# Loads of the first queries and key differences moved among the projections, hi and lo in one store, keys of two heads from ScalarE's queue

## The chip, the cores and the metric

The kernel runs on one core of a Trainium2 chip. The metric is the device time of one execution in microseconds. Three timed runs of the kernel before gave 1366.81, 1367.34 and 1368.3 us, a median of 1367.34.

## What is computed

The reference joins two results for a sequence of 2048 rows of 448 numbers, side by side. The first half is a state-space convolution: a kernel K is summed from complex exponentials and applied to `u` by FFT. The second half is attention with 16 heads of 28:

```python
K = 2.0 * jnp.einsum("dn,dnl->dl", C, P).real
y = jnp.fft.irfft(Uf * Kf[None, :, :], L2)[:, :, :L]        # then + u * D_skip
...
qkv = (x @ wqkv).reshape(B, S, 3, H, Dh).transpose(2, 0, 3, 1, 4)
scores = jnp.einsum("bhqd,bhkd->bhqk", q, k) * scale
o = jnp.einsum("bhqk,bhkd->bhqd", softmax(scores), v)
b = o.transpose(0, 2, 1, 3).reshape(B, S, D) @ wo
```

## The kernel before

The work has two parts. In the first (`for t in range(n_stage)`, line 515, 41 steps) the projections of `x` are computed beside the seeds of the exponentials. In the second (`for s in range(NS)`, line 980) attention, the powers of the exponentials and the FFT of the convolution run interleaved in an order written out by hand (`ORDER`, line 33).

**Projections.** `x` comes in four chunks of 512 rows (`load_x`, `transposes`). `qk_proj(c, s, g)` (line 440) multiplies chunk c by the weights of group g (four heads) for the keys (s = 1) or the queries (s = 0), in three products of split numbers each, 12 matmuls in all. Its result stands in one of three PSUM tiles (`w_tile`). The function `evac` that it returns splits the result: ScalarE writes the rounded part `th` (hi), VectorE the rest `tl` (lo), and SP stores both in DRAM, `k_d` or `q_d`. For the keys of the first two chunks it also makes the differences of two halves, `dh` and `dl`, and stores them in `kd_d`. There are 32 such jobs and 16 of `v_proj` (line 474). `project` (line 507) starts a job and then evacuates the one before it; PW = 37 spreads the 48 jobs over the first 37 steps. For the last chunk the v jobs come first, and then keys and queries of groups 0 to 3 by turns.

**Seeds.** `seeds(o)` (line 308), eight of them, four steps apart (SP = 4), each go through GpSimd, VectorE and ScalarE: `phases`, `reduce`, `sines`, `sizes`, `g_base`, `g_first` and so on. Their products `sg` and `se` are stored in `sd_d` (`put_g`, `put_e`). `se` is a buffer of the ring `qhat` with three buffers, which the queries use too (`places`, line 354).

**Loads for attention.** After the last projection (t + 1 == PW) the pool of the weights is closed (`wst.close()`, line 522) and the key pools are opened where it was. Then SP issues, in this order: `load_q(0)`, and for each of four heads `load_kd(0, j)` and `load_k(0, j)`; then `load_q(1)` and four `load_v`. Each of `load_k` (line 140), `load_kd` (line 154) and `load_q` (line 159) consists of four DMAs, one for each 32 partitions.

**First maxima.** Then the row maxima of the first 512 queries are computed (`max_mm`, line 166): 16 blocks, each with four matmuls. The first uses the key differences; ScalarE takes its positive part into `rl` (a tile of the pool `kd_p`), and VectorE joins it with the second and reduces the other two. `max_join`, `max_end` and `max_put` write the maximum into the queries, and the second part begins.

**Order.** In the first part the program's order on each engine is set by a scheduler at build time, which moves instructions; in the second, everything stays in the order written. SP issues DMAs in its order. Each DMA signals one of eight completion counters, taken in turn, and waits for the DMA that had this counter before.

Of the kernel before, what the change touches and what calls it, by code (L numbers as in the profile page):

```python
# [1 line left out]

# [5 lines left out]
F32 = mybir.dt.float32  # L8
F32R = mybir.dt.float32r
# [13 lines left out]
HG = H // G  # L23
CQ = 512
# [15 lines left out]
PS = 1  # L40
SGB, XB, XL = 2, 5, 4
K0, KP, KD, UP = 0, 3.5, 5, 3

N1 = 32
N2 = 64
# [43 lines left out]
def body(ctx, tc, a, out):  # L89
    nc = Engines(tc)  # L90
# [29 lines left out]
    att, k0_st = ExitStack(), ExitStack()  # L120
    ps_w, n_ring = [None, 3], [0]

    def w_tile():

        n_ring[0] += 1
        return ps_w[0].tile([128, CQ], F32, name=f"pm{n_ring[0] % ps_w[1]}")

    q_p = pool(att, "q_p", side="right")
    v_p = pool(att, "v_p", side="right")

    def mm32(o, w, x_, start, stop, at=0):

        for i in range(w.shape[-1] // 32):
            c = slice(32 * i, 32 * i + 32)
            nc.tensor.matmul(o[c], w[:, c], x_, start=start, stop=stop, tile_position=(0, at + 32 * i))


    kt_g, kd_g, q_u, m_u, mh_u, o_u, rl_u = {}, {}, {}, {}, {}, {}, {}

    def load_k(g, j, p):  # L140
        t = p.tile([128, L], F32R, name="khat", bufs=HG)
        for r in range(4):
            nc.sync.dma_start(t[32 * r:32 * r + 32, :].bitcast(F32), k_d[g][r % 2, 32 * j:32 * j + 32, :])
        kt_g.setdefault(g, []).append(t)

    v_g = {}
# [1 line left out]
    def load_v(g, c):  # L148
        v_g[g, c] = t = v_p.tile([128, NK // NQ, HG, 32], F32, name="v", bufs=5)
        nc.sync.dma_start(t.rearrange("p t h e -> p t (h e)"), v_d[c][:, g])  # L150

    kd_p = [None]

    def load_kd(g, j):
        kd_g[g, j] = t = kd_p[0].tile([128, CQ], F32R, name=f"kdif{j}")
        for r in range(4):
            nc.sync.dma_start(t[32 * r:32 * r + 32].bitcast(F32), kd_d[g][r % 2, 32 * j:32 * j + 32, :])

    def load_q(u):
        g, c = divmod(u, NQ)  # L160
        t = q_p.tile([128, HG, CQ], F32R, name="qhat", bufs=3)
        for r in range(4):
            nc.sync.dma_start(t[32 * r:32 * r + 32].bitcast(F32), q_d[g][c][r // 2].rearrange("(j p) q -> p j q", j=HG))
        q_u[u] = t

    def max_mm(u, i, kc, ps=w_tile):

        if i == 0 and kc == 0:
            m_u[u] = q_p.tile([128, HG, 4, 3], F32, name="mx", bufs=2)
        j, t = divmod(i, 4)  # L170
        pm = ps()
        q, kt = q_u[u][:, j, t * 128:(t + 1) * 128], kt_g[u // NQ][j]
        mx = m_u[u][:, j, t, max(kc - 1, 0):max(kc - 1, 0) + 1]
        if kc == 0:
            nc.tensor.matmul(pm, q, kd_g[u // NQ, j], start=True, stop=True)
            rl_u[u, i] = kd_p[0].tile([128, CQ], F32, name="rl", bufs=2)
            nc.scalar.activation(rl_u[u, i], pm, AF.Relu)
        elif kc == 1:
            kb = kt.rearrange("p (c s n) -> p c s n", c=NQ, s=2)[:, :2, 1, :]
            nc.tensor.matmul(pm.rearrange("p (c n) -> p c n", c=2), q, kb, start=True, stop=True)  # L180
            rl = rl_u.pop((u, i))
            nc.vector.tensor_tensor_reduce(rl, pm, rl, 1.0, -3.0e38, ALU.add, ALU.max, mx)
        else:
            nc.tensor.matmul(pm, q, kt[:, kc * CQ:(kc + 1) * CQ], start=True, stop=True)
            nc.vector.tensor_reduce(mx, pm, axis=AX.X, op=ALU.max)
# [19 lines left out]
    with ExitStack() as st:  # L205
# [3 lines left out]
        x_p = pool(xst, "x_p")  # L209
        y_p = pool(wst, "y_p", side="right")  # L210
# [45 lines left out]
        t = a["A_log_dt"]  # L256
# [183 lines left out]
        def qk_proj(c, s, g):  # L440
            pp = w_tile()
            hs = slice(HG * g, HG * g + HG)
            n = 0
            for k in range(NCK):
                for w_, x_ in ((wh, xh), (wl, xh), (wh, xl)):
                    nc.tensor.matmul(pp, w_[:, s, k, hs, :].rearrange("p h e -> p (h e)"), x_[k],
                                     start=n == 0, stop=n == 3 * NCK - 1)
                    n += 1

            def evac():  # L450
                th = x_p.tile([128, CQ], F32R, name="th", bufs=2)
                tl = x_p.tile([128, CQ], F32R, name="tl", bufs=2)
                if s == 1:
                    nc.scalar.activation(th, pp, AF.Identity, bias=kones)
                    nc.vector.scalar_tensor_tensor(tl, pp, kones, th.bitcast(F32), op0=ALU.add, op1=ALU.subtract)
                else:
                    nc.scalar.activation(th, pp, AF.Copy)
                    nc.vector.tensor_tensor(tl, pp, th.bitcast(F32), ALU.subtract)
                if s == 1 and c < 2:
                    HC = CQ // 2  # L460
                    kb = y_p.tile([128, HC], F32, name="kb")
                    dh = y_p.tile([128, HC], F32R, name="dh")
                    dl = y_p.tile([128, HC], F32R, name="dl")
                    nc.scalar.activation(kb, pp[:, HC:], AF.Copy)
                    nc.vector.tensor_tensor(kb, pp[:, :HC], kb, ALU.subtract)
                    nc.scalar.activation(dh, kb, AF.Copy)
                    nc.gpsimd.tensor_tensor(dl, kb, dh.bitcast(F32), ALU.subtract)
                    for i, t in enumerate((dh, dl)):
                        nc.sync.dma_start(kd_d[g][i, :, c * HC:(c + 1) * HC], t.bitcast(F32))
                for i, t in enumerate((th, tl)):  # L470
                    nc.sync.dma_start(k_d[g][i, :, c * CQ:(c + 1) * CQ] if s == 1 else q_d[g][c][i], t.bitcast(F32))
            return evac

        def v_proj(c, t):
# [25 lines left out]
        slots = [[] for _ in range(n_stage)]  # L500
# [3 lines left out]
        slots[1].insert(0, turn_dt)  # L504
        pend, n_work = [], len(work)

        def project():

            e = work.pop(0)() if work else None
            while pend:  # L510
                pend.pop(0)()
            if e:
                pend.append(e)

        for t in range(n_stage):
            while work and n_work - len(work) < n_work * (t + 1) / PW:
                project()
            for f in slots[t]:
                f()
            if t + 1 == PW:  # L520
                project()
                wst.close()
                kd_p[0] = pool(att, "kd_p", side="right")
                k0_p = pool(k0_st, "k0_p", side="right")
                load_q(0)
                for j in range(HG):
                    load_kd(0, j)
                    load_k(0, j, k0_p)
                load_q(1)
                for c in range(NQ):  # L530
                    load_v(0, c)
# [188 lines left out]
    def fin(u, s_):  # L720
# [15 lines left out]
        def scale():  # L736
            pw = w_tile()
            for t in range(4):
                mm32(pw[:, t * 128:(t + 1) * 128], rb[:, t].rearrange("p h e -> p (h e)"), ident, True, True)
            nc.vector.tensor_tensor(on, o, pw, ALU.mult)  # L740
            if g < G - 1:
                nc.sync.dma_start(on_d[c][g], on)
            else:
                p_due.extend((s_ + PD + PS * t, lambda t=t: project(t)) for t in range(4))
# [107 lines left out]
        for kc in range(4):  # L852
            max_mm(1, i, kc)

    import collections
    urgent, back = collections.deque(), collections.deque()
    powers = {"g": collections.deque(), "e": collections.deque()}
    done = {"mm": -1}
# [121 lines left out]
    for s in range(NS):  # L980
        u, kt = divmod(s, NK)
# [57 lines left out]
    s = NS  # L1039
# [63 lines left out]
```

## Time and profile before

| what | value |
|---|---|
| median of three timed runs | 1367.34 us |
| the profiled execution | 1366.65 us |
| its span, first to last instruction | 1364.9 us |
| busy: PE, DVE, ACT, POOL | 1243.5, 980.3, 968.6, 831.0 us |
| mean granted clock of TensorE | 0.975 |
| DMA moved | 205.37 MB, mean 150 GB/s |

The page gives busy time by engine, the same in 40 slices of the span with the granted clock, the chain of work that ended last, and the costliest groups of instructions. All of the program's operations are recorded by one helper, so that they all have line 73; they are told apart by the names of their tiles: `th` and `tl` for the evacuations, `qhat`, `kdif` and `khat` for the loaded queries, key differences and keys, `mx` for the maxima, `tri`, `sg` and `px` for the seeds. SPq is the queue SP, with the DMAs that it issues.

### The profile page before, as it was taken

What the parts mean: (1) busy time and instruction counts of PE and PEld (TensorE: products, weight loads), DVE (VectorE), ACT (ScalarE), POOL (GpSimd) and SP (SyncE); (2) the same over time, 40 slices, a digit from 0 to 9 for tenths busy, and PEclk for the clock granted to TensorE, in tenths of its full rate; (3) what the DMA queues carried; (4) which work ended last, traced back from release to release, by engine and by line L of the source; (5) the groups of instructions that cost most, each with busy time, mean ns of one, the idle gap of its engine ahead of it and who ended that gap; (6) DMA issues with size and microseconds to landing.
All of it is one profiled execution on the core that took longest, in us unless ns stands there. A gap on an engine that the chain in (4) does not pass through costs nothing.

```text
span 1364.9 us, 33230 instructions
## 1 busy us (share of the span) xinstructions
PE 1243.5 (91%) x12625; PEld 707.2 (52%) x12625; DVE 980.3 (72%) x2138; ACT 968.6 (71%) x2069; POOL 831.0 (61%) x705
## 2 busy tenths in 40 slices
PE   6978784799999999999999999999998999998997
PEld 4866662355555555555555555555555545544433
DVE  5778765877777777777788888887887766857311
ACT  4867662488888888888888888878786665655553
POOL 3576661187877877878878988888896111202221
PEclk9988896999999999999999999999999999999999
DMA  6775679726675546378533233632324544636476
GB/s 194 241 243 193 219 263 246 208 62 140 160 168 119 131 125 155 109 205 209 161 96 88 64 72 78 148 86 66 77 66 139 181 123 154 208 109 205 138 192 178
DMA packets 200729, 205.37 MB, mean 150 GB/s; under 512 B 96632, under 2 KB 159160, under 8 KB 198520
## 3 DMA queue, kind: packets, MB, share of 16 engines
q1 hardware_dynamic: 200568, 203.23, 53.5%
q8 instruction: 100, 1.64, 0.5%
q14 instruction: 61, 0.50, 0.1%
HBM read 120.73 MB, written 82.18 MB: 149 GB/s over the span
## 4 chain that ended last, share of the span: by engine, by line
PE 58%; DVE 16%; ACT 11%; POOL 5%; DMA 5%; issue 3%; SPq 0%; ACTq 0%; DVEq 0%; POOLq 0%
PE pm L73 34%; PE po L73 13%; PE pss L73 12%; ACT p L73 6%; DVE mx L73 3%; POOL qhat L73 3%; DVE g L73 2%; ACT rl L73 2%; DVE p L73 2%; DMA khat<-k 2%; DVE tri L73 1%; DVE pr L73 1%; DVE px L73 1%; POOL x_e L73 1%; DVE sg L73 1%
## 5 line engine op out<-in xcount | busy, mean ns | idle before, releaser
L73 ACT ACTIVATE p<-pss 128x512 f32<-128x512 f32 x1024 | 565.3, 608 | 137.0 <-PE pss L73 128.4
L73 PE MATMUL pss<-qhat,khat 128*128 128x512 f32 x1024 | 402.2, 399 | 3.5 <-ACT p L73 3.4
L73 DVE TENSOR_REDUCE mx<-pm 128x1 f32<-128x512 f32 x500 | 321.4, 683 | 104.6 <-PE pm L73 103.4
L73 PE MATMUL pm<-khat,qhat 128*128 128x512 f32 x749 | 329.7, 443 | 41.5 <-DVE mx L73 36.1
L73 POOL TENSOR_TENSOR e<-e,sdb 128x256 f32<-128x256 f32 x168 | 201.9, 1202 | 166.0 <-ACT e L73 157.0
L73 PE MATMUL po<-p,v 128*32 128x512 f32 x2048 | 271.8, 598 | 0.0
L73 POOL TENSOR_TENSOR e<-e,eu 128x256 f32<-128x256 f32 x168 | 248.5, 1479 | 13.2
L73 PEld LDWEIGHTS pm<-khat,qhat 128*128 128x128 f32 x749 | 141.0, 189 | 217.7 <-DVE mx L73 83.4
L73 PEld LDWEIGHTS pss<-qhat,khat 128*128 128x128 f32 x1024 | 190.6, 188 | 45.9 <-issue 11.1
L73 DVE CUSTOM_DVE_ANT_0 rl<-pm,rl 128x512 f32<-128x512 f32 x249 | 171.5, 689 | 47.3 <-ACT rl L73 44.2
L73 POOL TENSOR_TENSOR eu<-e,sdb 128x256 f32<-128x256 f32 x168 | 201.8, 1201 | 0.0
L73 DVE TENSOR_TENSOR g<-g,zg 128x128 f32<-128x128 f32 x392 | 162.9, 416 | 46.6 <-ACT zg L73 41.5
L73 ACT ACTIVATE rl<-pm 128x512 f32<-128x512 f32 x249 | 150.8, 606 | 24.9 <-PE pm L73 24.9
L73 POOL TENSOR_TENSOR p<-pr,pr 64x448 f32<-64x448 f32 x32 | 40.9, 1277 | 191.7 <-DVE pr L73 180.6
L73 PE MATMUL pm<-kdif,qhat 128*128 128x512 f32 x249 | 100.9, 405 | 2.4 <-DMA v<-v 1.3
L73 PEld LDWEIGHTS pm<-e,g 128*32 128x32 f32 x3584 | 63.0, 110 | 52.8 <-issue 30.9
L73 DVE TENSOR_TENSOR zg<-g,zg 128x128 f32<-128x128 f32 x224 | 87.5, 391 | 1.9
L73 PEld LDWEIGHTS po<-p,v 128*32 128x32 f32 x2048 | 56.5, 110 | 42.6 <-issue 37.9
L73 PE MATMUL pm<-e,g 128*32 128x64 f32 x3584 | 72.5, 220 | 0.0
L73 ACT ACTIVATE y<-pm 128x448 f32<-128x448 f32 x48 | 26.3, 548 | 63.5 <-PE pm L73 30.9
L73 PE MATMUL pm<-xh,wh 112*128 112x512 f32 x128 | 56.2, 443 | 11.2 <-DVE tl L73 5.1
L73 DVE TENSOR_TENSOR pr<-pm,ub 128x448 f32<-128x448 f32 x64 | 37.0, 619 | 32.7 <-PE pm L73 32.7
(137 smaller groups left out, 1555.4 us busy)
## 6 DMA issues: line engine op xcount, KB each, us to landing
sdb<-sd SPq DMA_DIRECT2D x56, 336.0 KB
qhat<-q SPq DMA_DIRECT2D x64, 256.0 KB
khat<-k SPq DMA_DIRECT2D x64, 256.0 KB
sd<-sg SPq DMA_DIRECT2D x8, 1456.0 KB
mw<-in_mw SPq DMA_DIRECT2D x16, 512.0 KB
sd<-qhat SPq DMA_DIRECT2D x8, 896.0 KB
yk<-yk SPq DMA_DIRECT2D x56, 128.0 KB
yu_d<-ub SPq DMA_DIRECT2D x64, 112.0 KB
```

The costliest lines, as they stand in the source:

```text
L73: i = f(*args, **kw)
```

## The change

Four edits. The pool `kd_p` is opened at the start, with room of its own, so that `load_kd` can be called before the weights' pool is closed. The 16 DMAs of the first group's key differences are issued two at a time in steps 26 to 33, and the four of the first queries in steps 34 and 35. Hi and lo share one tile, `hl` (differences: `dhl`), and go out in one DMA of twice the size. The keys of heads 0 and 1 of the first group are issued by ScalarE, those of heads 2 and 3 by SP as before.

```diff
+A0, A1 = 26, 34
...
+    kd_p = pool(att, "kd_p", side="right")
...
-    def load_k(g, j, p):
+    def load_k(g, j, p, queue=nc.sync):
         t = p.tile([128, L], F32R, name="khat", bufs=HG)
         for r in range(4):
-            nc.sync.dma_start(t[32 * r:32 * r + 32, :].bitcast(F32), k_d[g][r % 2, 32 * j:32 * j + 32, :])
+            queue.dma_start(t[32 * r:32 * r + 32, :].bitcast(F32), k_d[g][r % 2, 32 * j:32 * j + 32, :])
...
-    def load_kd(g, j):
-        kd_g[g, j] = t = kd_p[0].tile([128, CQ], F32R, name=f"kdif{j}")
-        for r in range(4):
+    def load_kd(g, j, rows=range(4)):
+        if 0 in rows:
+            kd_g[g, j] = kd_p.tile([128, CQ], F32R, name=f"kdif{j}")
+        t = kd_g[g, j]
+        for r in rows:
...
-    def load_q(u):
+    def load_q(u, rows=range(4)):
...
-                th = x_p.tile([128, CQ], F32R, name="th", bufs=2)
-                tl = x_p.tile([128, CQ], F32R, name="tl", bufs=2)
+                hl = x_p.tile([128, 2, CQ], F32R, name="hl", bufs=2)
+                th, tl = hl[:, 0], hl[:, 1]
...
-                    for i, t in enumerate((dh, dl)):
-                        nc.sync.dma_start(kd_d[g][i, :, c * HC:(c + 1) * HC], t.bitcast(F32))
-                for i, t in enumerate((th, tl)):
-                    nc.sync.dma_start(k_d[g][i, :, c * CQ:(c + 1) * CQ] if s == 1 else q_d[g][c][i], t.bitcast(F32))
+                    nc.sync.dma_start(kd_d[g][:, :, c * HC:(c + 1) * HC].rearrange("i p l -> p i l"), dhl.bitcast(F32))
+                nc.sync.dma_start((k_d[g][:, :, c * CQ:(c + 1) * CQ] if s == 1 else q_d[g][c]).rearrange("i p l -> p i l"),
+                                  hl.bitcast(F32))
...
+        ahead = collections.defaultdict(list)
+        for i in range(2 * HG):
+            ahead[A0 + i].append(lambda i=i: load_kd(0, i // 2, range(2 * (i % 2), 2 * (i % 2) + 2)))
+        for i in range(2):
+            ahead[A1 + i].append(lambda i=i: load_q(0, range(2 * i, 2 * i + 2)))
...
-            for f in slots[t]:
+            for f in slots[t] + ahead.get(t, []):
                 f()
             if t + 1 == PW:
                 project()
                 wst.close()
-                kd_p[0] = pool(att, "kd_p", side="right")
                 k0_p = pool(k0_st, "k0_p", side="right")
-                load_q(0)
                 for j in range(HG):
-                    load_kd(0, j)
-                    load_k(0, j, k0_p)
+                    load_k(0, j, k0_p, nc.scalar if j < 2 else nc.sync)
                 load_q(1)
```

More of the change, by code (lines that the diff above doesn't have):

```diff
@@ L1 @@
+import collections
 from contextlib import ExitStack
@@ L150, in load_v @@
         nc.sync.dma_start(t.rearrange("p t h e -> p t (h e)"), v_d[c][:, g])
-    kd_p = [None]
-    def load_kd(g, j):
-        kd_g[g, j] = t = kd_p[0].tile([128, CQ], F32R, name=f"kdif{j}")
-        for r in range(4):
+    def load_kd(g, j, rows=range(4)):
[3 more added lines that the diff above has]
+        for r in rows:
             nc.sync.dma_start(t[32 * r:32 * r + 32].bitcast(F32), kd_d[g][r % 2, 32 * j:32 * j + 32, :])
-    def load_q(u):
+    def load_q(u, rows=range(4)):
         g, c = divmod(u, NQ)
-        t = q_p.tile([128, HG, CQ], F32R, name="qhat", bufs=3)
-        for r in range(4):
+        if 0 in rows:
+            q_u[u] = q_p.tile([128, HG, CQ], F32R, name="qhat", bufs=3)
+        t = q_u[u]
+        for r in rows:
             nc.sync.dma_start(t[32 * r:32 * r + 32].bitcast(F32), q_d[g][c][r // 2].rearrange("(j p) q -> p j q", j=HG))
-        q_u[u] = t
     def max_mm(u, i, kc, ps=w_tile):
@@ L175, in max_mm @@
             nc.tensor.matmul(pm, q, kd_g[u // NQ, j], start=True, stop=True)
-            rl_u[u, i] = kd_p[0].tile([128, CQ], F32, name="rl", bufs=2)
+            rl_u[u, i] = kd_p.tile([128, CQ], F32, name="rl", bufs=2)
             nc.scalar.activation(rl_u[u, i], pm, AF.Relu)
@@ L461, in evac @@
                     kb = y_p.tile([128, HC], F32, name="kb")
-                    dh = y_p.tile([128, HC], F32R, name="dh")
-                    dl = y_p.tile([128, HC], F32R, name="dl")
+                    dhl = y_p.tile([128, 2, HC], F32R, name="dhl")
+                    dh, dl = dhl[:, 0], dhl[:, 1]
                     nc.scalar.activation(kb, pp[:, HC:], AF.Copy)
@@ L853, in body @@
             max_mm(1, i, kc)
-    import collections
     urgent, back = collections.deque(), collections.deque()
```

## The prediction

> **What bounds the kernel now.** I read the page first (span and slices), then the busy time by stretch, and then the timeline of the stretch where the slices show a hole.
>
> ```profile
> span 1364.9 us, 33230 instructions
> PE   6978784799999999999999999999998999998997
> PEclk9988896999999999999999999999999999999999
> ```
>
> From the ninth slice on TensorE is at 9 tenths in almost every slice, with an order written out by hand that the change doesn't touch. I take that part, from about 255 us to the end, as a block that starts earlier or later and keeps its length. The first eight slices (34 us each) are not full, and the hole is in the seventh (4 tenths, the clock at 6). Busy time by stretch (columns: stretch and its length, PE, PEld, DVE, ACT, POOL busy with counts, granted clock, DMA share, GB/s):
>
> ```profile
> 180.00:200.00 20.00, 18.64 (x71) 14.31 (x71) 15.35 (x29) 14.09 (x30) 12.20 (x17) 0.91 0.93 322
> 200.00:212.00 12.00, 0.00 (x0) 0.00 (x0) 7.73 (x19) 2.24 (x7) 5.42 (x9) 0.69 0.53 182
> 212.00:224.00 12.00, 1.62 (x3) 0.93 (x4) 0.00 (x0) 1.08 (x2) 4.18 (x5) 0.50 1.05 250
> 224.00:238.00 14.00, 12.52 (x31) 6.24 (x31) 13.18 (x29) 3.58 (x6) 0.00 (x0) 0.84 1.04 237
> ```
>
> TensorE does nothing from 200 to 212 us and almost nothing to 224, while the DMA engines are full from 212 on. The timeline says who waits (start, duration, engine, operation; in brackets the idle time before and what ended it):
>
> ```profile
> 199.23 0.40 PE L73 MATMUL pm<-xl,wh 112*128 112x512 f32 x1
> 201.65 0.66 POOL L73 TENSOR_TENSOR tri<-tri 128x224 f32<-128x224 f32 x1
> 202.34 0.56 DVE L73 TENSOR_TENSOR sg<-pn,tri 128x224 f32<-128x224 f32 x1 [5.25 <-POOL tri L73]
> 206.95 0.55 DVE L73 TENSOR_TENSOR sg<-sg,px 128x224 f32<-128x224 f32 x1
> 207.69 0.68 ACT L73 ACTIVATE th<-pm,kones 128x512 fp32r<-128x512 f32 x1
> 210.84 0.32 SPq L73 DMA_DIRECT2D q<-tl  x1
> 211.22 1.87 SPq L73 DMA_DIRECT2D qhat<-q  x4
> 213.18 1.76 SPq L73 DMA_DIRECT2D kdif<-kd  x4
> 215.04 3.23 SPq L73 DMA_DIRECT2D khat<-k  x4
> 219.17 0.79 PE L73 MATMUL pt<-kdif,qhat 128*128 128x512 f32 x1 [19.54 <-DMA kdif<-kd]
> 223.60 0.76 PE L73 MATMUL pt<-khat,qhat 128*128 128x512 f32 x1 [3.20 <-DMA khat<-k]
> 224.52 0.69 DVE L73 CUSTOM_DVE_ANT_0 rl<-pt,rl 128x512 f32<-128x512 f32 x1 [13.44 <-PE pt L73]
> 246.74 0.50 PE L73 MATMUL pm<-kdif,qhat 128*128 128x512 f32 x1 [1.30 <-DMA v<-v]
> 254.97 0.20 DVE L73 TENSOR_REDUCE m<-mx 128x16 f32<-128x48 f32 x1
> ```
>
> The last projection is multiplied by 199.6, but ScalarE copies it out only at 207.7: it stands behind the copies of the last seed (`sg`), these behind VectorE's chain (202.34 to 207.50), and that behind GpSimd's `tri`. The last stores are issued until 210.84, and only then the queue SP reaches the loads. The maxima start on VectorE at 224.52 and end at 254.97; they are VectorE's pace, 48 passes in 30.45 us, with one stall of 1.3 us for a load. So the stretch that the change works on is 199 to 224.5, and what counts is the time of that first maximum.
>
> **The change part by part.** It was made against the built order of both programs (which instruction stands behind which on each engine, and which completion it waits for), with durations of this profile. The profiled execution took 1366.65 us, 1.75 over its span; the median of the three timed runs is 1367.34. My sum is made against 1366.65.
>
> *First queries and key differences earlier.*
>
> ```profile
> qhat<-q SPq DMA_DIRECT2D x64, 256.0 KB
> kdif<-kd SPq DMA_DIRECT2D x16, 64.0 KB
> sd<-sg SPq DMA_DIRECT2D x8, 1456.0 KB
> sd<-qhat SPq DMA_DIRECT2D x8, 896.0 KB
> 193.07 0.37 SPq L73 DMA_DIRECT2D sd<-sg  x1
> 203.86 0.39 SPq L73 DMA_DIRECT2D sd<-qhat  x1
> ```
>
> 4 issues (1.87 us) and 16 issues (1.76 each four) leave the hole for earlier places on SP. Of what stood ahead of the first head's keys, the issues from 211.22 to 215.04, 3.8 us, go. Their 2.1 MB (4 x 256 and 16 x 64 KB) move earlier: at the 250 GB/s of the row from 212 on that is 8.4 us of transfer, in a stretch that ends with a DMA share of 0.93 (180 to 200). The cover is the DMA engines' idle share; where it is gone, stores land later, and that is the last item of this part. Two things spoil the gain. The last two quarters of the queries don't get away: the DMAs take eight completion counters in turn, and the third quarter has the counter of the first key piece, so it is issued only when that has landed. And the stores of the last seed but one, 2.4 MB that are issued at 193.07 and 203.86 now, stand in the new order of SP behind the stores of the last projections but two, so they fall into the hole. At the 322 GB/s of 180 to 200 they take 7.5 us there.
>
> *Keys by ScalarE.* In the built order the first two pieces of head 0 stand before ScalarE's last two evacuations, the third between them, the fourth and head 1 after. The first waits for the last-but-one multiplication of the last projection, whose weights lie where the keys go. Behind it on ScalarE are two evacuations and the `rl` copies; the first maxima wait for those, and for the keys anyway.
>
> *What moves with it.* In the new order the evacuations of the last four projections are behind the last seed's copies too, so TensorE can't finish at 199.6: the last projection needs the PSUM tile that is freed by the third evacuation from the end. Clock and pitch for that:
>
> ```profile
> 202.00:204.00 2.00, 0.00 (x0) 1.00 0.00 0
> 226.00:228.00 2.00, 2.00 (x6) 0.50 0.98 206
> 228.00:230.00 2.00, 1.89 (x6) 0.91 1.11 286
> 196.90 0.40 PE L73 MATMUL pm<-xh,wl 112*128 112x512 f32 x1
> ```
>
> Eleven matmuls from 196.90 to 199.23 are 0.233 us apart; the granted clock is still 1.00 at 202 to 204, 0.50 from 212 on (row above), and back only at 228, four us after the steady work began. Now step by step. GpSimd's `tri` comes before the seed's other products in the new order (two of 0.40 and one of 0.42 stood ahead of it), so 201.65 becomes about 200.4 and it ends at 201.1. VectorE's chain of 5.2 us (202.34 to 207.50) then ends at 206.3, with the evacuation that frees the last-but-one projection inside it, at about 205.5. That projection runs cold, 12 x 0.46 = 5.5 us, to 211.0; the last, whose tile is free by 208.5, runs 12 x 0.233 = 2.8 us warm, to 213.8. Both pitches are the 0.233, at half clock doubled. First key piece at 213.9 and second, 0.32 each as a lone issue; evacuation 0.68; third piece; evacuation; fourth piece issued by 216.5. It lands 3.2 us later if it goes as a lone store does (136.42 to 139.66 in the rows below), or 5.3 later as the fourth piece does now (issued by 218.27, used at 223.60). VectorE follows 0.9 after that (223.60 to 224.52). That gives a first maximum at 220.6 or 222.7, against 224.52. Now 2.3 MB are issued in the 7 us up to that piece; in the new order it is some 3 MB in 8 us (two merged stores, the seed's 1.5 MB, half of the queries, the keys). So I take a value nearer to the late end, 222.0: 2.5 us earlier. The stall of 1.3 us goes as well: the fourth head's keys have 2.1 MB of loads fewer ahead of them, and each head feeds VectorE for 7 us. **Gain in the hole: 3.8 us**; ends 5.2 (early landing, stall gone) and 1.8 (late landing, stall stays).
>
> *One store for hi and lo.* 64 stores of keys and queries and 16 of differences become 40: 40 x 0.32 = 12.8 us less of SP, which is not on the chain. What it costs is a wait. The two halves share one tile of two buffers, so ScalarE's hi of the next but one projection waits for a store that waits for VectorE's lo. Now hi waits for hi alone:
>
> ```profile
> 70.54 0.60 ACT L73 ACTIVATE th<-pm 128x512 fp32r<-128x512 f32 x1
> 72.16 0.38 SPq L73 DMA_DIRECT2D q<-tl  x1
> 134.25 0.32 SPq L73 DMA_DIRECT2D q<-tl  x1
> 135.40 0.58 ACT L73 ACTIVATE th<-pm 128x512 fp32r<-128x512 f32 x1
> 136.42 0.94 SPq L73 DMA_DIRECT2D k<-th  x1
> 138.35 0.47 SPq L73 DMA_DIRECT2D k<-tl  x1
> 138.71 0.69 DVE L73 TENSOR_TENSOR tl<-pm,th 128x512 fp32r<-128x512 f32 x1 [0.85 <-DMA q<-tl]
> 139.66 0.69 ACT L73 ACTIVATE th<-pm,kones 128x512 fp32r<-128x512 f32 x1 [0.43 <-DMA k<-th]
> ```
>
> Two landing times stand here: 3.2 us (136.42 to 139.66) and 4.4 (134.25 to 138.7). The hi at 70.54 would have to wait for the lo stored at 72.16, that is to 76.6 at most, 6.0 us; that at 135.40 to 138.7, 3.3; that at 139.66 to 141.6, 1.9. Bounds: about 11 us of held ScalarE if all lands on the chain, nothing if its idle time takes it (it is busy 14.09 of 20 us in the row above). Behind a held hi stand the sines and copies of the seeds, on which GpSimd and VectorE wait. The nearest row is that of the table of waits from 18 to 215 us:
>
> ```profile
> ACT th L73 <- DMA k<-th: 1.4, 2, 0.9
> ```
>
> This is what ScalarE loses by stores of hi today (total, times, longest). **I take 1.4 us more**, this loss once again: the pairs at 70 and 135 us are the worst that I found, and ScalarE has idle time behind them.
>
> **Sum:** 1366.65 - 3.8 + 1.4 = 1364.25, so 1364.2 us, 3.1 under the median shown.
>
> The Trainium skill has a rule against one edit (DMA: Bandwidth & Descriptors, "Issuing engines are not separate DMA queues"): transfers from ScalarE and SP run on the same 16 DMA engines and interleave, so a second issuer saves issue time alone. The DMA share of 1.05 and 1.04 in the rows from 212 to 238 agrees; by that rule the keys of heads 2 and 3 could slow head 0. In the built order they stand behind the last store and behind pieces of heads 0 and 1, so my sum has no term for it; its result is the first rival.
>
> **Rivals.**
>
> 1. *The hole only changes its owner.* Keys still can't leave before the last projection is done, which is then 14 us later than 199.6; the last query quarters wait behind the first key piece, the seed's stores fill the DMA engines, and the stall in the loop stays. First maximum at 222.7: 1366.65 - 1.8 + 1.4 = 1366.2, no difference. For it speaks that the DMA engines are full from 212 on already; against it, that 2.1 MB of what fills them are moved away. That the first queries aren't loaded ahead as the change says is a part of this case.
>
> 2. *The merged store holds ScalarE (slower).* Place: the bursts of projections about 70 and 135 us; price up to 11.2 us, against a gain of 3.8. It decides from 7.3 us on: 1366.65 - 3.8 + 7.3 = 1370.1; at the full price 1374.0. For it: GpSimd's, VectorE's and ScalarE's parts of a seed form one chain with no slack at 202 (5.25 us of VectorE waiting for GpSimd), and ScalarE runs in order. Against it: ScalarE has 6 of 20 us idle (14.09 busy), and the like waits cost 1.4 us now.
>
> **How the numbers follow.** A measurement of this kernel can tell about 0.2% (2.7 us) from no change: faster is below 1364.6, slower above 1370.1. My forecast has 0.52, with its own range of 1360.5 (the early end of the gain, and a microsecond from the shorter SP queue) to 1366.2; 0.43 of it lies below 1364.6, since the late landing is in its value already, and 0.09 above. Rival 1 has 0.14, all of it within 0.2%. Rival 2 has 0.34, all of it above 1370.1. That makes 0.43, 0.23 and 0.34. The range goes from 1359.5, for a phase that also gets shorter by the 40 issues saved, to 1372.5, which takes in the nearer two thirds of rival 2.
>
> **What would show it.** Right: the first maximum on VectorE at 222 plus the 1.4 us of held ScalarE, no stall near the fourth head, `m<-mx` at about 252.6. TensorE's last projections cold and about ten us later than now, with `khat` issued by ScalarE between the last evacuations. Wrong: GpSimd's last `tri` later than 201.65 (then the projections, not the hole, took the time; look at ScalarE's waits for stores), or a first maximum that is earlier but a loop that stalls (rival 1). If the stretch from 255 us on changes its length, my block assumption fails.

## The result: 5.4 us slower, and the profile after

The changed kernel takes 1372.21 us, the median of ten runs (1368.84 to 1375.94), beside 1366.79 for ten runs of the kernel before. The ratio is 1.0036, with a 95% interval of 1.0025 to 1.0047. The profiled execution took 1372.32 us. The ratio is the one on record; it isn't the plain quotient of the two medians.

The page of the changed kernel: the span, TensorE's busy tenths and its granted clock.

```profile
span 1370.5 us, 33146 instructions
PE   7877775799999999999999999999998999998997
PEclk9988986899999999999999999999999999999999
```

The hole in the seventh slice is still there, a little less deep (5 tenths for 4). Busy time of the four stretches that the prediction showed (columns as there):

```profile
180.00:200.00 20.00, 16.22 (x67) 12.62 (x65) 13.90 (x28) 13.91 (x24) 12.47 (x16) 0.91 0.52 178
200.00:212.00 12.00, 6.25 (x21) 4.98 (x22) 8.82 (x21) 4.05 (x14) 5.55 (x11) 0.72 0.76 247
212.00:224.00 12.00, 1.07 (x5) 0.54 (x3) 1.44 (x2) 1.28 (x2) 5.24 (x6) 0.66 1.03 309
224.00:238.00 14.00, 10.20 (x21) 5.68 (x21) 7.98 (x17) 3.19 (x6) 0.00 (x0) 0.56 1.06 296
```

TensorE now works from 200 to 212 us (the last projections), as foreseen. But the DMA engines are full until 238 as before, now at 309 and 296 GB/s where it was 250 and 237: bytes were to leave the hole, and more are in it. VectorE has 7.98 us of work from 224 to 238, where it had 13.18. The timeline of the changed kernel (ACTq is the queue ScalarE):

```profile
200.75 0.65 POOL L75 TENSOR_TENSOR tri<-tri 128x224 f32<-128x224 f32 x1
205.75 0.79 PE L75 MATMUL pm<-xh,wh 112*128 112x512 f32 x1 [5.97 <-DVE hl L75]
210.47 0.50 SPq L75 DMA_DIRECT2D sd<-sg  x1
212.67 0.40 PE L75 MATMUL pm<-xl,wh 112*128 112x512 f32 x1
212.87 1.56 ACTq L75 DMA_DIRECT2D khat<-k  x2
214.56 1.10 ACTq L75 DMA_DIRECT2D khat<-k  x1
215.81 10.24 ACTq L75 DMA_DIRECT2D khat<-k  x5
219.83 1.02 SPq L75 DMA_DIRECT2D qhat<-q  x2
227.25 0.77 PE L75 MATMUL pt<-kdif,qhat 128*128 128x512 f32 x1 [14.18 <-DMA khat<-k]
228.91 1.29 DVE L75 TENSOR_REDUCE mx<-pm 128x1 f32<-128x512 f32 x2 [11.81 <-PE pm L75]
252.05 0.50 PE L75 MATMUL pm<-kdif,qhat 128*128 128x512 f32 x1 [1.31 <-DMA v<-v]
260.28 0.20 DVE L75 TENSOR_REDUCE m<-mx 128x16 f32<-128x48 f32 x1
```

Up to 213 us this is the prediction within about a microsecond. Then the 1456-KB store of the last seed but one (`sd<-sg`) goes out 2.4 us ahead of the first key piece. That piece, issued at 212.87, has landed by 219.83, since the third query quarter, which waits for its counter, is issued then: 7.0 us. The last two quarters are needed at 227.25, some 7 us after their issue. (The row names `khat` as what ended the wait, but this matmul reads `kdif` and `qhat`. The trace also holds the time of every counter's increments: by them the first key piece was complete at 219.81, the fourth at 223.28, and the last query quarter, issued at 220.52, at 227.01. So the queries end the wait, whatever the row names.) The first maximum is at 228.91 in place of 224.52, 4.4 us later; the stall of 1.3 us for a load (252.05) is still there; the loop ends 5.3 us later (260.28 for 254.97); the span is 5.6 us longer.

Behind the loop both kernels do the same work. Busy time by stretch there, first of the kernel before, then of the changed one (the third figure from the right is the granted clock):

```profile
254.00:260.00 6.00, 4.41 (x10) 2.20 (x10) 4.41 (x12) 1.20 (x2) 0.00 (x0) 0.72 0.26 76
260.00:266.00 6.00, 4.79 (x14) 2.18 (x14) 3.79 (x9) 4.08 (x8) 0.00 (x0) 1.00 0.84 215
266.00:272.00 6.00, 4.54 (x27) 2.03 (x26) 5.90 (x14) 4.82 (x11) 5.41 (x7) 1.00 0.67 140
1234.00:1240.00 6.00, 5.85 (x46) 2.89 (x47) 2.35 (x6) 1.85 (x4) 0.00 (x0) 0.72 0.26 66
```

```profile
260.00:266.00 6.00, 5.46 (x11) 2.79 (x11) 4.42 (x12) 1.19 (x2) 0.00 (x0) 0.51 0.37 112
266.00:272.00 6.00, 5.73 (x14) 3.33 (x13) 3.21 (x8) 4.20 (x9) 0.00 (x0) 0.63 0.83 195
272.00:278.00 6.00, 4.63 (x16) 2.15 (x17) 4.67 (x12) 3.34 (x8) 5.53 (x7) 0.72 0.60 123
1234.00:1240.00 6.00, 4.02 (x40) 1.99 (x38) 5.06 (x8) 3.53 (x7) 3.83 (x3) 1.00 1.04 374
```

The changed kernel runs cold for longer after the loop (0.51, 0.63, 0.72), and the same ScalarE instructions, matched one by one, are then 7.4 us behind instead of 5.3; near 1235 us the kernel before falls to half clock once (0.72) and the changed one doesn't, and 1.7 us come back. What I took for a block has joints.

### The profile page after: what moved, and what is told of

Same layout as the page of the kernel before. It is cut to its first block, busy times and chain, and to the rows that moved or that the text cites. A ratio compares the mean times of both kernels' runs of the same rounds, so it can differ in the third digit from the quotient of the medians.

```text
span 1370.5 us, 33146 instructions
## 1 busy us (share of the span) xinstructions
PE 1242.8 (91%) x12625; PEld 709.0 (52%) x12625; DVE 990.5 (72%) x2138; ACT 969.2 (71%) x2069; POOL 824.7 (60%) x705
## 4 chain that ended last, share of the span: by engine, by line
PE 61%; DVE 16%; ACT 11%; DMA 4%; issue 3%; POOL 3%; SPq 0%; ACTq 0%; DVEq 0%; POOLq 0%
PE pm L75 36%; PE po L75 13%; PE pss L75 12%; ACT p L75 6%; DVE mx L75 3%; DVE tri L75 2%; DVE g L75 2%; ACT rl L75 2%; DVE p L75 2%; POOL qhat L75 2%; DVE pr L75 1%; DMA khat<-k 1%; DVE sg L75 1%; DVE px L75 1%; DVE zg L75 1%
## 5 line engine op out<-in xcount | busy, mean ns | idle before, releaser
L75 ACT ACTIVATE y<-pm 128x448 f32<-128x448 f32 x48 | 26.3, 547 | 62.0 <-issue 30.3
```

The lines of the kernel that those rows point to most:

```text
L75: i = f(*args, **kw)
```

## The experiments

Three theories stood at the start. **Store:** the 1456-KB store ahead of the keys fills the DMA engines, so that everything behind it lands late. **Counter:** the last two query quarters wait for a key piece's counter. **Merged store** (second rival of the prediction): the shared tile holds ScalarE. A fourth came with the first traces: **held VectorE**, below. All results (times in us; *tri* is the start of GpSimd's last triangle product, *first* that of VectorE's first maximum, *end* that of `m<-mx`, all in the profiled execution; *rest* is span minus *end*; *cold* the time at half clock in the rest, in the trace's clock record, where each stretch that lies wholly in it is a multiple of 3.4 us). The medians of e1 to e14 come from three chips, on which the kernel before made 1366.97 to 1367.63; the ratio compares runs of one chip and is the better guide:

| kernel | median | ratio to before, 95% | tri | first | end | rest | cold |
|---|---|---|---|---|---|---|---|
| before | 1366.79 | | 201.65 | 224.52 | 254.97 | 1109.9 | 10.2 |
| changed | 1372.21 | 1.0025 to 1.0047 | 200.75 | 228.91 | 260.28 | 1110.2 | 18.0 |
| e1 queries earlier | 1375.88 | 1.0050 to 1.0092 | 197.11 | 225.79 | 258.58 | 1111.8 | 19.8 |
| e2 stores deferred | 1366.50 | 0.9984 to 1.0009 | 198.61 | 222.65 | 252.99 | 1110.1 | 10.3 |
| e3 keys by SP | 1373.42 | 1.0035 to 1.0059 | 197.94 | 229.18 | 259.63 | 1112.8 | 20.5 |
| e4 before + merged store | 1373.85 | 1.0030 to 1.0056 | 205.00 | 231.53 | 261.99 | 1112.1 | 19.8 |
| e5 clamp from PSUM | 1372.55 | 1.0023 to 1.0052 | 196.44 | 224.86 | 256.71 | 1114.0 | 20.5 |
| e6 e2 + e5 | 1362.45 | 0.9956 to 0.9979 | 195.56 | 218.72 | 249.07 | 1111.6 | 16.0 |
| e7 two stores again | 1374.66 | 1.0044 to 1.0070 | 200.84 | 230.37 | 261.94 | 1112.8 | 20.5 |
| e8 changed, again | 1371.64 (one) | | 198.33 | 227.16 | 258.66 | 1111.1 | 18.8 |
| e9 short seed store | 1365.24 | 0.9989 to 1.0009 | 201.56 | 225.57 | 255.91 | 1110.2 | 16.5 |
| e10 before + early loads | 1375.98 | 1.0052 to 1.0079 | 199.89 | 232.09 | 262.55 | 1112.1 | 20.0 |
| e11 before + ScalarE's keys | 1368.15 | 1.0000 to 1.0017 | 200.12 | 221.89 | 254.17 | 1109.9 | 14.0 |
| e12 before + clamp from PSUM | 1368.13 | 0.9995 to 1.0015 | 200.22 | 224.87 | 255.72 | 1110.6 | 16.5 |
| e13 e4 + clamp from PSUM | 1363.78 | 0.9956 to 0.9980 | 199.52 | 221.62 | 252.08 | 1110.0 | 10.2 |
| e14 e9 + clamp from PSUM | 1366.20 | 0.9974 to 1.0000 | 198.40 | 222.49 | 252.83 | 1113.5 | 20.5 |

Every edit lets the build-time scheduler order the first part anew, so a variant is never the edit alone; where the order matters, the text says so.

### e1: the counter alone

```diff
-A0, A1 = 26, 34
+A0, A1 = 26, 30
```

> The changed kernel with the four pieces of the first queries issued in steps 30 and 31 in place of 34 and 35. In the built order all four are then ahead of the first key piece, and none has its completion counter. Main theory (the last two query quarters are issued only when the first key piece has landed, 219.8 us, and the first maximum waits for them): the first maximum then waits for head 0's keys alone, which were complete at about 223.3, so it comes at about 224.3 in place of 228.9, and the time is 1372.2 - 4.6 = 1367.6 us. Second theory (the 1456-KB store ahead of the keys decides, through bytes alone): the first key piece still takes about 7 us to land, 219 to 220, and the first maximum is between 224 and 227. Rival (the merged store of hi and lo takes the time before 213): nothing moves, first maximum at 229, 1372.

The queries were there in time, and the median is 3.7 us above that of the changed kernel, where 4.6 less was expected. The six executions go from 1372.19 to 1382.79, and the profiled one is the fastest of them. The timeline of e1:

```profile
207.65 0.44 SPq L75 DMA_DIRECT2D sd<-sg  x1
213.12 1.66 ACTq L75 DMA_DIRECT2D khat<-k  x2
215.39 0.69 ACT L75 ACTIVATE hl<-pm,kones 128x512 fp32r<-128x512 f32 x1 [5.93 <-DMA k<-hl]
216.70 11.33 ACTq L75 DMA_DIRECT2D khat<-k  x6
224.99 0.77 PE L75 MATMUL pt<-khat,qhat 128*128 128x512 f32 x1 [6.14 <-DMA khat<-k]
```

The first maximum now waits for the keys. Their second half is issued only at 216.70, since ScalarE's evacuation ahead of it waits until 215.39 for a merged store that was issued at 209.18 behind the seed's store, and it lands 8 us later. From *tri* to *first* it is 28.7 us, in the changed kernel 28.2. But *tri* is a poor start for the hole: the first key piece is issued 16.0 us after it in e1 (213.12) and 12.1 in the changed kernel (212.87). From that issue to *first* it is 12.7 us in e1 and 16.0 in the changed kernel. So the counter is worth some 3 us of the hole itself, although both stores of the seed stand ahead of the keys in e1; this order lost them again ahead of the hole and in the loop (*first* to *end* 32.8 for 31.4).

### e2 and e9: the store

e2 issues both stores of that seed behind the keys of all heads:

```diff
+        held = slots[SP * 6 + 11][:1] + slots[SP * 6 + 12][:1]
+        del slots[SP * 6 + 11][:1], slots[SP * 6 + 12][:1]
...
                     load_k(0, j, k0_p, nc.scalar if j < 2 else nc.sync)
+                for f in held:
+                    f()
                 load_q(1)
```

> The changed kernel with the two stores of the last seed but one (1456 and 896 KB) issued after the loads of all four heads' keys. The queries' third and fourth quarter get other counters by it; the fourth key piece gets that of the first. Store theory (the 1456-KB store that is issued 2.4 us ahead of the first key piece holds the DMA engines): the first key piece lands 3 to 4 us after its issue in place of 6.9, at about 216.5; the fourth is issued at about that time and lands by 220; first maximum at 221, time 1364.5. If only the shared counter matters and the landing stays at 7 us: the fourth key piece is issued at 219.8 and lands at 224 to 226, first maximum at 225 to 227, time 1368 to 1370. Rival (merged store): 1372.

e9 leaves the store in its place and makes it a third (the rest of that seed's `sg` is left out, and the second part reads the seed before it in its place):

```diff
-            put_g = lambda: nc.sync.dma_start(sd_d[o][:, :, F_G:].rearrange("b p f -> p b f"), q["sg"])
+            put_g = lambda w=128 if o == 6 else None: nc.sync.dma_start((sd_d[o][:, :, F_G:F_G + w] if w else sd_d[o][:, :, F_G:]).rearrange("b p f -> p b f"),
+                                              q["sg"][:, :, :w] if w else q["sg"])
...
-        nc.sync.dma_start(sds[b], sd_d[b // BO][b % BO])
+        nc.sync.dma_start(sds[b], sd_d[5 if b // BO == 6 else b // BO][b % BO])
```

> The changed kernel, but of the last seed but one only 128 of 364 columns of sg are stored (512 KB in place of 1456), and the second part reads the seed before it in its place; work is left out by that, and the result is another one. The store stays where it is, ahead of the keys; the last two query quarters get counters of the queries' first quarter and of a store. Theory of the store's bytes: key pieces land in under 5 us as with the deferred stores (6.9 us in the changed kernel), GpSimd's last triangle product to first maximum 24 to 25 us (28.2 and 28.8 in two profiles of the changed kernel), time 1366 to 1369. If the place of the store or its counter matters and not its bytes: 28 us and 1372.

The two timelines, e2 first:

```profile
208.33 1.61 SPq L75 DMA_DIRECT2D qhat<-q  x2
211.86 0.82 ACTq L75 DMA_DIRECT2D khat<-k  x2
216.68 3.90 ACTq L75 DMA_DIRECT2D khat<-k  x5
221.42 0.77 PE L75 MATMUL pt<-khat,qhat 128*128 128x512 f32 x1 [5.40 <-DMA khat<-k]
```

```profile
211.28 0.55 SPq L75 DMA_DIRECT2D sd<-sg  x1
211.88 2.70 SPq L75 DMA_DIRECT2D qhat<-q  x2
215.13 0.83 ACTq L75 DMA_DIRECT2D khat<-k  x2
220.90 3.01 ACTq L75 DMA_DIRECT2D khat<-k  x5
224.34 0.77 PE L75 MATMUL pt<-khat,qhat 128*128 128x512 f32 x1 [3.73 <-DMA khat<-k]
```

In both the fourth key piece has the first one's counter, so its issue shows the first landing: 4.8 us after issue in e2 (211.86 to 216.68), 5.8 in e9. Then 4.7 and 3.4 us until TensorE reads them. Two landings in a row again, but shorter ones: from *tri* to *first* 24.0 us in both, 4.2 less than in the changed kernel, the stall in the loop is gone (*first* to *end* 30.3 against 31.4), and the time goes from 1372.2 to 1366.5 and 1365.2. In e2 the fourth key piece's wait for the first one's counter kept the first maximum at 222.65, not the 221 of the store theory.

**The store theory is not shown by these two alone.** In both, the last two query quarters also got other counters and went out ahead of the keys (the `qhat` rows above), so the counter's part is in their gain too. And the second profile of the changed kernel, e8, speaks against the bytes of the first landing:

```profile
208.06 0.52 SPq L75 DMA_DIRECT2D sd<-sg  x1
211.92 1.57 ACTq L75 DMA_DIRECT2D khat<-k  x2
217.73 1.02 SPq L75 DMA_DIRECT2D qhat<-q  x2
```

With the whole 1456 KB issued 3.9 us ahead, the first key piece landed in 5.8 us (counter record), and with 512 KB 3.9 us ahead, in e9, in 5.7; e6, with neither store ahead, has 6.2. The nine profiles with early queries and ScalarE's keys sort better by the counter. From the issue of the first key piece to *first* it is 15.2 to 16.9 us where the last quarters wait for it (changed kernel, e5, e7, e8), 12.7 in e1, where they don't but both stores stand ahead, and 10.4 to 11.2 where they don't and the store is short or behind (e2, e6, e9, e14). So of the some 5 us about 3 go with the counter and about 2 with the stores; the second figure, like the first, leans on the one order of e1.

### e4, e7, e10, e11, e3: the parts one at a time

e4 is the kernel before with the merged store alone, e10 with the early loads alone, e11 with ScalarE's keys alone; e7 and e3 are the changed kernel without the first and without the last.

> The kernel before with nothing but the merged store of hi and lo. Rival theory of the prediction (the merged store holds ScalarE in the bursts of projections and the seeds' chain comes late): GpSimd's last triangle product later than 201.65 and 1368 to 1374 us. By the other theories it costs next to nothing there and leaves SP fewer issues at the end (the last stores' two and the wait between them, about 1 us): 1365.5 to 1367.

> The kernel before with the early loads of the first queries and key differences alone (two stores for hi and lo, all keys by SP). Its built order, too, has the last seed but one's stores just ahead of the keys, and the keys behind the last projection's stores. By the theory of the stores in the hole: first maximum at 228 to 231, 1371 to 1375 us. If the early loads do what they are for and another part of the change costs the time: first maximum before 223, under 1365.

> The kernel before with nothing but the keys of heads 0 and 1 by ScalarE. Here the 1456-KB store of the last seed but one is far ahead of the keys, the 896-KB one close to them, and the first queries stand behind the last projection's stores with counters of key pieces. If queue SP's order decides: the queries are the last to come, first maximum at 224 to 228, 1366 to 1371. If a second issuing engine helps by itself: first maximum at 222 or earlier, 1364.

```diff
-                hl = x_p.tile([128, 2, CQ], F32R, name="hl", bufs=2)
-                th, tl = hl[:, 0], hl[:, 1]
+                th = x_p.tile([128, CQ], F32R, name="th", bufs=2)
+                tl = x_p.tile([128, CQ], F32R, name="tl", bufs=2)
...
```

> The changed kernel with hi and lo in two tiles and two stores again, early loads and ScalarE's keys kept. If the merged store is what shifts GpSimd's work so that VectorE is held: no held clamp, executions within 4 us as with the kernel before. The hole has the same stores and counters in it, and the first part is that of the kernel before: first maximum at 227 to 229, 1369 to 1372 us. If the merged store alone makes the change slower: 1366 or less.

```diff
-                    load_k(0, j, k0_p, nc.scalar if j < 2 else nc.sync)
+                    load_k(0, j, k0_p)
```

> The changed kernel with all keys of the first group issued by SP. They then stand behind the last stores, the 896-KB one among them, and the last query quarters get away at about 213, without a key piece's counter. By the counter theory the queries are there by 220; the keys are issued from about 217.5 (last store) to 219 and land 3 to 7 us later; first maximum at 223 to 226, time 1366.5 to 1369.5, which is earlier than with ScalarE's help. If issuing by ScalarE is what brings the keys early and the queries don't matter: first maximum later than 229, time above 1372.

The early loads alone cost 9 us (e10), the merged store alone 6 to 7 (e4), ScalarE's keys alone about 1, with the first maximum 2.6 us earlier than before and 32.3 us from *first* to *end* where before has 30.4 (e11). e4 came out as the second rival had it, e10 a little beyond what the store theory had. So the early loads are slower by themselves than all three together; for the merged store the intervals overlap. Whether ScalarE's keys win back part of what the early loads lose is not clear of the noise (e3 beside the changed kernel, e7 beside e10). e7, which was to take 1369 to 1372 us, took 1374.66 with no held clamp (the longest 1.74 us): its last query quarters wait for key pieces' counters as in the changed kernel, so the long hole doesn't need the merged store. The timeline of e3, with all keys by SP:

```profile
210.97 0.40 PE L75 MATMUL pm<-xl,wh 112*128 112x512 f32 x1
212.29 1.43 SPq L75 DMA_DIRECT2D sd<-qhat  x1
213.81 2.04 SPq L75 DMA_DIRECT2D q<-hl  x1
228.23 0.79 PE L75 MATMUL pt<-khat,qhat 128*128 128x512 f32 x1 [8.49 <-DMA khat<-k]
```

Keys stand behind the 896-KB store and the last projection's store and are used at 228.23, 16.9 us after the last projection's last matmul ended; in the changed kernel TensorE starts again 14.2 us after it. In e3 the queries had no key's counter and were early (as expected), but the keys took their place, and I had their landing too short again. The miss in e11 was the other way: the early end of the hole came with queue SP's order against it, and the loop gave 1.8 us of it back.

### e5, e6, e8, e12, e13, e14: a held VectorE instruction

In the first part, the clamp of the phase (one 128 x 112 instruction on VectorE for each of eight seeds) took, by its group row (count, busy time in all, mean ns, idle time ahead), before and then after:

```profile
L73 DVE TENSOR_SCALAR tri<-tri 128x112 f32<-128x112 f32 x8 | 6.8, 846 | 0.1
```

```profile
L75 DVE TENSOR_SCALAR tri<-tri 128x112 f32<-128x112 f32 x8 | 18.4, 2304 | 0.1
```

One of the eight makes the difference. The timeline of the changed kernel there:

```profile
104.52 1.03 POOL L75 TENSOR_TENSOR qhat<-qhat 128x336 f32<-128x336 f32 x1
104.70 9.76 DVE L75 TENSOR_SCALAR tri<-tri 128x112 f32<-128x112 f32 x1
105.49 1.03 POOL L75 TENSOR_TENSOR x_e<-qhat 128x336 f32<-128x336 f32 x1
...
113.20 1.19 POOL L75 TENSOR_TENSOR qhat<-tri 128x112 f32<-128x112 f32 x3
```

and of its second profiled execution (e8, the same kernel):

```profile
105.34 1.03 POOL L75 TENSOR_TENSOR qhat<-qhat 128x336 f32<-128x336 f32 x1
105.53 0.92 DVE L75 TENSOR_SCALAR tri<-tri 128x112 f32<-128x112 f32 x1
```

The clamp begins 0.2 us into a GpSimd instruction both times. Once it gets through when that one ends; once it waits for eleven of them, until GpSimd has no more (114.39), and ends 0.07 us later. The Trainium skill (SBUF — State Buffer, "SBUF: two separate sides") says that VectorE in a two-port mode and GpSimd share a pair of ports under an exclusive lock, and that whoever starts first has it for the whole instruction. The trace agrees that one blocks the other (0.92 and 9.76 us for an instruction of 0.21), and shows more: the one that waits can be passed over many times. e5 takes the operand from PSUM:

```diff
-                vec.scalar_tensor_tensor(t0, k0, MAGIC, im, op0=ALU.subtract, op1=ALU.subtract)
-                vec.tensor_scalar(t0, t0, 0.5, -0.5, op0=ALU.min, op1=ALU.max)
+                vec.scalar_tensor_tensor(im, k0, MAGIC, im, op0=ALU.subtract, op1=ALU.subtract)
+                vec.tensor_scalar(t0, im, 0.5, -0.5, op0=ALU.min, op1=ALU.max)
```

> The changed kernel with the clamp of the phase (VectorE, 128 x 112, 0.21 us where nothing disturbs it) reading PSUM in place of SBUF, in all eight seeds. In the profiled execution of the changed kernel one of these eight took 9.76 us (104.70 to 114.46), just as long as GpSimd had instructions in a row without a gap; in the profile of the kernel before the longest took 1.74. Theory of the held VectorE: this costs about 5 us in some executions of the kernels with the merged store, and not in others, which is why ten executions of the changed kernel lie 7 us apart. Without it: no such instruction over 2.5 us, GpSimd's last triangle product 2 to 4 us before 200.75, first maximum at 225 to 227, executions within 4 us, median 1368.8. If it has no part in the difference: the same scatter and 1372.

> The changed kernel once more, for a second profiled execution. If VectorE is held in some executions only, this one shows either the held clamp again at 104.7 and a time of 1372 to 1376, or no held clamp, GpSimd's last triangle product at about 197 to 198.5, the first maximum at 224 to 226.5 and a time of 1368.5 to 1370.5. In both the stretch from that product to the first maximum is about 28 us: the hole doesn't depend on it.

> Both mends together: the clamp reads PSUM, and the two stores of the last seed but one are issued after the keys' loads. If the slower time is the sum of two causes (VectorE held in some executions, about 3 us in the median; the hole before the first maximum 4 us longer through stores ahead of the keys and counters shared with them): first maximum at 221 to 223, 1363 to 1365 us, executions within 4 us, which is under the kernel before. If the two are one cause, no better than the second mend alone, 1366.5.

> The kernel before with the clamp reading PSUM: the control for the second mend. In its profile no clamp takes over 1.74 us (0.21 undisturbed), so it should gain at most a microsecond or two: 1365 to 1367. If it comes out near 1362.5 as the changed kernel with both mends does, that gain has nothing to do with the change.

> The kernel before with the merged store and the clamp reading PSUM. The merged store alone made 1373.9 us; its profile had a clamp of 9.75 us at 105.05, GpSimd's last triangle product 3.4 us later than in the kernel before, and ScalarE's last evacuation 3.3 us behind a store. If the held clamp is the price of the merged store in the first part: no clamp over 2.5 us, the product at 200 to 202, 1369.5 to 1371 (the wait for the store stays). If the product stays at 205 without a held clamp: the merged store makes the first part longer in another way, 1373 to 1374.

> The changed kernel with the short store of the last seed but one (512 of 1456 KB, so that work is left out) and the clamp reading PSUM. The short store alone made 1365.2. If the clamp's gain shows wherever the hole is not filled by the store, as with the deferred stores (1366.5 to 1362.5): 1361 to 1363. If that gain belonged to that one kernel's order: 1365.

The group row of e5 (it takes in the other 128 x 112 instruction that reads PSUM, 0.27 us each in the kernel before too):

```profile
L75 DVE TENSOR_SCALAR tri<-pn 128x112 f32<-128x112 f32 x16 | 4.3, 266 | 1.1 <-ACT tr L75 1.0
```

No clamp is held any more, and *tri* comes at 196.44. In the five profiles with this edit no clamp takes over 0.29 us. So it is shown that the clamp is held when it reads SBUF beside GpSimd and not when it reads PSUM; that the ports are the reason rests on the Trainium skill alone. e8 was to take 1368.5 to 1370.5 us without a held clamp, and took 1371.64; the twelve executions of e5 were to lie within 4 us, and lie within 8.4. The worth of the clamp is not one number. In e13 the merged store with this clamp takes 1363.8 us where e4 took 1373.9; e4 had a held clamp of 9.75 us, and its *tri* was 5.5 us later (205.00 for 199.52). That gains more than the 1369.5 to 1371 expected: from *tri* to *first*, too, it is 4.4 us less, where the new order has no evacuation behind a store (3.3 us in e4). Beside the deferred stores it is worth 4 us (e6, 1362.45 where 1363 to 1365 was expected), in the kernel before nothing (e12, 1368.13 where 1365 to 1367 was expected), beside the short store nothing that is clear of the noise (e14), and in the changed kernel nothing (e5). In the profiles of these last two the first maximum is 3.1 and 4.1 us earlier than without it, and the gain is lost after the loop: *rest* is 1114.0 in e5 and 1113.5 in e14, the two longest, with 20.5 us at half clock each. e8, without a held clamp, is 1.75 us ahead at the first maximum and only 0.8 at the end. My claim that the held clamp was some 3 us of the median's 5.4 fell with e5.

e6 and e13 are both faster than the kernel before, by 0.2 to 0.4%.

## Why the prediction was wrong, step by step

**The phase to 213 us: right, by luck in part.** *tri* at 200.4, the last-but-one projection freed at 205.5, the last ending at 213.8, the first key piece at 213.9; measured 200.75, 205.75, 213.1 (212.67 + 0.40), 212.87. The order was read rightly. The times held because a held clamp, which the prediction didn't know, stood against a first part that is otherwise shorter: without it *tri* comes 2 to 4 us earlier and the first key piece 1.0 (e8) and 3.4 (e5).

**The landing of the fourth key piece, as what ends the hole: the step that failed.** The prediction gave it 3.2 or 5.3 us after an issue at 216.5 and let VectorE follow 0.9 later, 222.0. The issue was right (the third group of the queue ScalarE begins at 215.81). The landing was too short: it took 7.5 us, to 223.28. And it is not what ends the hole, since the wait of the last query quarters was put at nothing. Two landings of 7 us in a row end it: first key piece, 212.87 to 219.81, then the last query quarter, complete at 227.01; VectorE begins 1.9 later, at 228.91. Of the 6.9 us beyond 222.0, 2.2 are the fourth key piece's, 3.7 the query quarters' behind it, and 1.0 the last step's. Both facts stood in the prediction, the shared counter and the 2.4 MB of seed stores with 7.5 us, as things that "spoil the gain", and neither became a term of the sum. The 3.2 us was read from a lone store in a free stretch. The bytes by which the late end was preferred are also added up wrong: two merged stores, the seed's 1.5 MB, half of the queries and the keys (1.0, 1.5, 0.5 and 1.0 MB) are some 4 MB in 8 us, not 3. e2 and e9 show what the counter and the store are worth together: 5.2 and 5.6 us from the first key piece's issue on, and 1.0 of the loop.

**The stall of 1.3 us in the loop: wrong.** It stays (1.31). The argument was that 2.1 MB fewer stand ahead of the loads; 2.4 MB more stand there. Where the stores go (e2) it goes.

**The merged store: sign right, size and place wrong.** ScalarE's waits for stores, by the table of waits of the changed kernel from 18 to 215 us (total, times, longest):

```profile
ACT hl L75 <- DMA q<-hl: 2.4, 2, 1.4
ACT hl L75 <- DMA k<-hl: 0.9, 1, 0.9
```

3.3 us in place of 1.4; the 1.4 more that I took were 1.9. But alone it costs 6 to 7 us (e4), and its profile has a held clamp of 9.75 us in a place that the prediction didn't look at: VectorE behind GpSimd at 105 us. By e8 the same program may or may not meet it. The second rival's sign and its span of 1370.1 to 1374.0 hold for e4; for the whole change the place that decided was another, the hole.

**The hole only changes its owner (first rival): half right.** It did, and it got 4.4 us longer, where the rival had it 1.8 shorter.

**The block from 255 us: wrong by up to 4 us.** *rest* goes from 1109.9 to 1114.0 over 16 profiles of the same work. The long ones are those with more time at half clock: the four with 14 us or less have 1109.9 to 1110.1, the seven with 19.8 us or more 1111.8 to 1114.0. The joints are two places near 1050 and 1235 us and the one after the loop. For the change itself the block is off by 0.3 us in the two profiles, which is luck: 2.1 us were lost after the loop and 1.7 came back near 1235.

**Keys by ScalarE beside SP.** The rule of the Trainium skill that the prediction quotes, that transfers of both queues share the DMA engines, was weighed for heads 2 and 3 and not for the seed's store. ScalarE's first piece took 6.9 us with SP's store 2.4 us ahead of it and 4.8 in e2 with the store behind it; 5.8 in e8 and 6.2 in e6 show that the store isn't all of this.

What stays open: why the clamp's mend gains 4 us in one order and none in another beyond the clock's part; how counter and store share the hole beyond the one order of e1, since no run frees the counter and moves nothing else, or moves the store and leaves the counter; why e1's median is above that of the changed kernel; and how often the held clamp comes in runs that were not profiled.

## What to carry to other kernels

A load moved out of a hole doesn't shorten the hole if half of it is left waiting behind a counter, or if the scheduler lets a larger store in: list what every queue has in flight ahead of the transfer that ends the wait, in bytes, and price the landing in that company, not by a lone one. Where two DMAs share a completion counter, write the wait as a term: one more landing in series. And don't take a long stretch as rigid when the clock can fall in it; here it gave and took 2 us at a time.

## What the hardware showed beyond that

- One VectorE instruction of 0.21 us took 9.76 us while GpSimd ran eleven instructions without a gap (9.75 in the profiles of e4 and e9); from PSUM it was never held, 0.29 us at most in five profiles.
- The granted clock changes in steps of 3.4 us: the stretches at half clock behind the loop are 3.41, 6.83 or 10.24 us long where the span doesn't cut them. With the same instructions after the loop, 10.2 to 20.5 us at half clock were seen, and the time of that part moved by 4.1 us.
- The first 256-KB load of ScalarE's queue landed 6.9 us after its issue with 1456 KB issued 2.4 us ahead of it on another queue, 5.8 with 1456 KB 3.9 us ahead (e8), 5.7 with 512 KB 3.9 us ahead (e9), and 4.8 and 6.2 with neither (e2, e6): the size of the one store ahead doesn't fix it.
- The name that a row gives for what ended a wait can be that of another DMA: the trace's landing times of the counters showed the query quarters where the row named the keys.
